# Pair 2's blocks fetched in step 4, queries and values loaded two steps later, batch 1's M a step later

## The chip, the cores and the metric

The kernel runs on one core of a Trainium2 chip. The metric is the device time of one execution in microseconds. Five engines work side by side, each through its own list of instructions in order: TensorE (PE, whose weight loads are shown apart as PEld), VectorE (DVE), ScalarE (ACT), GpSimd (POOL) and SyncE (SP). SP does no arithmetic here; it issues the DMAs.

## The reference

Two attentions follow each other: 32 packed rows for each head attend to the keys and values, and the queries attend to the packed result. Its output is the input of a two-layer block whose gate is `h * clip(h + 3, 0, 6) / 6`.

```python
def sm_attn(qq, kk, vv):
    s = scale * np.matmul(qq, kk.transpose(0, 1, 3, 2))
    s = s - np.max(s, axis=-1, keepdims=True)
    a = np.exp(s)
    a = a / (np.sum(a, axis=-1, keepdims=True) + 1e-09)
    return np.matmul(a, vv)
p_packed = sm_attn(p, k, v)
out = sm_attn(q, p_packed, p_packed)      # 8 batches, 8 heads, 576 rows, 64 wide
...
h = x @ w_in                              # x: 4608 x 512, w_in: 512 x 2048
relu6 = np.clip(h + 3.0, 0.0, 6.0)
g = h * relu6 / 6.0
return (g @ w_out).astype(np.float32)     # w_out: 2048 x 512
```

## The kernel before

**Tiling.** The eight batches are worked one after the other. The second attention's last product and the first layer are joined: with `A` the second attention's weights, `x @ w_in = A @ (p_packed @ w_in)`, and the product in brackets is called M. It is made in four quarters of 512 columns (`u_m`, tiles `m_hi` and `m_lo`: every number is kept as a rounded high part and a low rest). `first_product` (L930) multiplies M with `a_hi` and `a_lo` into `ps_hh`; ACT and DVE form the gate `t` or `tb` from it (`gate_into`, L946), ACT casts and DVE or POOL subtracts to get high and low parts (`parted`, L957), and PE multiplies them with the second layer's weights into `acc` (`product`, L975; its matmuls stand on L977).

**Steps.** From batch 1 on, a batch has two chunks (`c`) of 16 steps (`f`), one for each 128 hidden columns; `s = 16 * c + f` counts them through. Two neighbouring steps make a pair. For seven of the eight pairs (`PAIRS = 7`) the second product is done with seven half-width products in place of eight (`pair_product`, L1185), in the manner of Strassen, for which three combined weight blocks per pair, T1, T2 and T4, are kept ready in tiles `wt`. They are made once, during batch 1 and its turn to batch 2 (`combine`, L1068).

**Slots.** The `wt` tiles have room for the blocks of four pairs only. `PLACE` gives each pair its slot: pairs 2, 5 and 6 share slot 0, pairs 0 and 4 slot 1. Those five pairs' blocks are stored to `t_kept` in DRAM and fetched again, 768 KB each, by `fetch_t` (L1114, its DMA on L1115) in the steps that `FETCHES` names as (step, pair), one list for each chunk. In the first chunk the pairs come in the order 5, 4, 3, 2, 1, 0, 6. So pair 2's fetch waits until PE has done pair 5's product, and PE's product of pair 2 waits for the fetch. A pair's product is put behind the first products of the following pair (`pend`, `second`).

**The next batch's inputs.** While batch `b` is worked, `attention_inputs` (L566), one piece a step from step 0, loads the next batch's packed rows, keys, first two query blocks and values, and has DVE turn the keys (`turn`, L561). A block is four DMAs (`load_blocks`, L296, its DMA on L301). `nat`, the landing place of blocks, has two buffers, and `tr`, where the turned ones go, four. `attention` follows from step 6 (batch 1) or 10. `STAGES` sets these starts.

**M of the next batch.** The weights `w_in` are stored once to `w_kept`; `first_quarters` (L1418) fetches the quarters 2, 1 and 0 of them again into one single buffer (`w_again`, L1416) and makes M's quarters (`soon`, from step 21); the fourth is fetched at step 31 and used early in the next batch (`late`). The values `v_nat` use the same buffer.

**What sets the order.** The lists above only give the order in which the program is written and what a piece may not be put ahead of (`issue_after`, `behind_gates`). From batch 1 on a scheduler puts each engine's instructions in order by a time line of its own, SP's DMAs too. Once in order, an engine doesn't pass over an instruction that waits.

Of the kernel before, what the change touches and what calls it, by code (L numbers as in the profile page):

```python
# [34 lines left out]
TURN_LAST = (12, 12, 12, 13, 13, 14, 15)  # L35


FETCHES = (((5, 2), (7, 0), (11, 6)), ((5, 2), (7, 4), (11, 5)))
EDGES = (1, 2, 3)


# [43 lines left out]
def packed_attention_moe(  # L85
# [141 lines left out]
    def rest(*parts):  # L227
        for part in parts:
            for _ in part:
                pass  # L230

    def coarse(part):

        for stop in part:
            if stop is None:
                yield
# [59 lines left out]
    def load_blocks(src, b, a):  # L296
        t = ap.tile([P, T, 32], F32, name="nat", tag="nat", bufs=2)
        for h in range(2):
            for c in range(2):
                r = 64 * h + 32 * c  # L300
                nc.sync.dma_start(  # L301
                    out=t[r:r + 32],
                    in_=src[b, 2 * a + h, :, 32 * c:32 * c + 32].rearrange("(t i) j -> i t j", i=32),
                )
        return t
# [10 lines left out]
    def load_p(b):  # L316
        nat = ap.tile([P, NPAIR, NPK], F32, name="p_nat", tag="pn", bufs=1)
        for h in range(2):
            for c in range(2):
                r = 64 * h + 32 * c  # L320
                nc.sync.dma_start(
                    out=nat[r:r + 32],
                    in_=p[b, :, :, 32 * c:32 * c + 32].rearrange("(a h) i j -> h i a j", h=2)[h],
                )
        state["p", b] = nat

    def transpose_p(b):
        t = ap.tile([P, NPAIR, NPK], F32, name="p_tr", tag="pt", bufs=1)
        nc.vector.transpose(out=t, in_=state.pop(("p", b)))
        state["p", b] = t  # L330
# [90 lines left out]
    def load_v_low(b):  # L421

        home, tag = (wr, "w_in0") if steady else (wp, "v_nat")
        t = state["v", b] = home.tile([P, NPAIR, NST, D], F32, name="v_nat", tag=tag, bufs=1)
        for c in range(4):
            nc.sync.dma_start(out=t[:, :, c], in_=v[b].rearrange("(a x) r d -> x r a d", x=2)[0, c * P:(c + 1) * P])
        for x in range(2):
            load_v_rest(b, x)
# [107 lines left out]
    def u_m(b, *ns):  # L536
        def cols(n):
            return lambda a, half: w_in_sb[n][half, :, a]

        rounds = each_head(pps[b % 2], *(cols(n) for n in ns))  # L540
        yield
        for n, banks in reversed(list(zip(ns, rounds))):
            hi, lo = m_tiles(b, n)
            for x, ps in enumerate(banks):
                nc.scalar.copy(out=hi[:, x], in_=ps)
                yield 1
                nc.vector.tensor_sub(out=lo[:, x], in0=ps, in1=hi[:, x].bitcast(F32))
                yield

    def behind_gates():  # L550

        stack = ExitStack()
        for name in ("first", "relu", "gate"):
            if name in state:
                stack.enter_context(tc.issue_after(state[name].ins))
        return stack

    def load(which, b, a):
        state["nat", which, b, a] = load_blocks(k if which == "k" else q, b, a)

    def turn(which, b, a):  # L561
        t = ap.tile([P, T, 32], F32, name="tr", tag="tr", bufs=4)
        nc.vector.transpose(out=t, in_=state.pop(("nat", which, b, a)))  # L563
        state[which, b, a] = t

    def attention_inputs(b):  # L566

        load_p(b)
        load("k", b, 0)
        load("k", b, 1)  # L570
        yield
        transpose_p(b)
        turn("k", b, 0)
        load("k", b, 2)
        yield
        turn("k", b, 1)
        load("k", b, 3)
        yield
        turn("k", b, 2)
        load("q", b, 0)  # L580
        yield
        turn("k", b, 3)
        load("q", b, 1)
        load_v_low(b)
        yield
# [425 lines left out]
    def edge_product(acc, f, hi, lo, summed, first, last):  # L1011
# [11 lines left out]
        product(acc[:, H2:], lhs(2), block(i, "B22"))  # L1023

    def moe(b, chunks, fill):

        accs = {}
# [86 lines left out]
    def fetch_t(i):  # L1114
        nc.sync.dma_start(out=slots[PLACE[i]].rearrange("p a x m -> p (a x m)"), in_=t_kept[KEPT.index(i)])  # L1115
# [33 lines left out]
    def owed(count):  # L1149

        while ready and count:
            count -= 1
            ready.pop(0)()
            if edges:
                ready.append(edges.pop(0)())

    def moe_pairs(b, c, fill):

        last = PAIRS - 1
# [251 lines left out]
    def keep_w_in(n):  # L1411
        nc.sync.dma_start(out=w_kept[n], in_=w_in_sb[n].rearrange("p f a e -> p (f a e)"))

    def fetch_w_in(n):
        t = w_in_sb[n] = wr.tile([P, FPC, NPAIR, P], F32, name="w_again", tag="w_in0")
        nc.sync.dma_start(out=t.rearrange("p f a e -> p (f a e)"), in_=w_kept[n])  # L1416

    def first_quarters(b):  # L1418

        for n in range(NCH - 2, -1, -1):  # L1420
            fetch_w_in(n)
            yield
            yield
            yield from coarse(u_m(b, n))

    for b in range(1, B):
        more = b + 1 < B
        inputs, packed, ahead = (x(b + 1) if more else iter(()) for x in (attention_inputs, attention, u_s2))
        ahead = coarse(ahead)
        if b == 1:  # L1430
            late = coarse(part for n in range(1, NCH) for part in u_m(1, n))
            turned = [combine(i) for i in range(PAIRS)]
        else:
            late = coarse(u_m(b, NCH - 1))
        soon = first_quarters(b + 1) if more else iter(())

        def fill(c, f):
            s = c * NF + f
            with behind_gates():
                if b == 1:  # L1440
                    for _ in range(LATE[s] if s < len(LATE) else 0):
                        next(late, None)
                    if s == 0:
                        with tc.issue_after(state["stored"].ins):
                            for n in range(NCH):
                                keep_w_in(n)
                    for i in range(PAIRS - 1):
                        for _ in range(TURN[i].count(s)):
                            next(turned[i], None)
                else:  # L1450
                    if s > 0:
                        next(late, None)
                    for at, i in FETCHES[c]:
                        if f == at and (b, c, i) != (2, 0, PAIRS - 1):
                            fetch_t(i)
                    if b == 2:
                        for _ in range(TURN_LAST.count(s)):
                            next(turned[PAIRS - 1], None)
                if s >= 21:
                    next(soon, None)  # L1460
                if s == 31 and more:
                    rest(soon)
                    fetch_w_in(NCH - 1)
            with tc.issue_after(state["load"].ins), behind_gates():
                for chain, (start, count) in zip((inputs, packed, ahead), STAGES[b > 1]):
                    for _ in range(count if s >= start else 0):
                        next(chain, None)

        for c in range(2):
            if (b, c) == (1, 0):  # L1470
                moe(b, (c,), lambda f, c=c: fill(c, f))
                rest(*turned[:FIRST_PAIRS])
                roles.extend((3, 0, 1, 2))
            else:
                moe_pairs(b, c, lambda f, c=c: fill(c, f))
        if b == 1:
            rest(*turned[:PAIRS - 1])
# [31 lines left out]
```

## Time and profile before

| | |
|---|---|
| median of 3 runs | 720.52 us (720.29 to 721.84) |
| the profiled execution | 721.55 us |
| its span in the profile | 719.8 us |
| mean granted TensorE clock | 0.988 |
| DMA, 116.94 MB | mean 162 GB/s |

The span is what the profile shows of the profiled execution, from its first to its last instruction; the rest of the 721.55 us lies around it. In the prediction "us from the start" means from the start of the span. The batches from 2 on can be told apart in the time line by the two output DMAs (L1225) near their first steps, at 220.0, 300.2, 389.1, 468.7 and 558.8 us for batches 2 to 6.

### The profile page before, as it was taken

To read this page: it belongs to the slowest core of one execution; us is meant where nothing else is said; L and a number is where in the kernel's file an instruction comes from. 1 tells how busy PE (TensorE), PEld (TensorE's weight loads), DVE (VectorE), ACT (ScalarE), POOL (GpSimd) and SP (SyncE) were. 2 spreads that over 40 slices of the span, in tenths; PEclk is the share of its full clock that TensorE was granted. 3 is DMA by queue.
4 is the path that set the end of the run, shared out by engine and by line. 5 is a ranking of instruction groups with operands and counts; after the bars stand their busy time and mean duration, and the time that the engine had idled before them with its cause. 6 is when DMAs were issued, how large, how long until landed. Compare 5 with 4: busy or idle time off the path is not lost.

```text
span 719.8 us, 16493 instructions
## 1 busy us (share of the span) xinstructions
PE 691.9 (96%) x6014; PEld 599.8 (83%) x6014; DVE 552.8 (77%) x1227; ACT 436.8 (61%) x1042; POOL 364.5 (51%) x555
## 2 busy tenths in 40 slices
PE   7699999999999999999999999999999999999997
PEld 5487876788778888889898898889888898889996
DVE  4798688587999879876698778896688858986644
ACT  4798886555655656655466555566456655665543
POOL 1556642655444454574454444575634535467643
PEclk9699999999999999999999999999999999999999
DMA  9969953846247657564365756494544853532031
GB/s 277 321 167 274 208 131 145 241 106 179 76 160 166 158 169 253 135 189 88 115 249 144 191 112 223 153 208 114 130 162 162 180 146 138 201 132 89 30 109 68
DMA packets 200832, 116.94 MB, mean 162 GB/s; under 512 B 173616, under 2 KB 185392, under 8 KB 197168
## 3 DMA queue, kind: packets, MB, share of 16 engines
q1 hardware_dynamic: 200208, 115.70, 57.1%
q8 instruction: 47, 0.77, 0.4%
q14 instruction: 33, 0.27, 0.1%
q10 hardware_dynamic: 544, 0.20, 0.1%
HBM read 98.30 MB, written 17.56 MB: 161 GB/s over the span
## 4 chain that ended last, share of the span: by engine, by line
PE 72%; DVE 12%; DMA 8%; ACT 3%; issue 2%; SPq 2%; POOL 1%; DVEq 0%; ACTq 0%; POOLq 0%
PE acc L977 39%; PE ps_hh L937 19%; PE ps L357 4%; DMA wt<-t_kept 4%; PE ps_h L615 3%; DMA nat<-in_k_dram 2%; PE ps L977 2%; SPq L301 1%; PE ps L477 1%; DVE t L949 1%; DMA w_again<-w_kept 1%; DVE wt L1087 1%; DVE tr L563 1%; DMA raw_in<-in_moe_w_in_dram 1%; PE ps_t L686 1%
## 5 line engine op out<-in xcount | busy, mean ns | idle before, releaser
L955 POOL TENSOR_TENSOR gf<-tb,gf 128x256 fp32r<-128x256 f32 x87 | 74.2, 853 | 124.2 <-ACT gf L954 85.9
L937 PE MATMUL ps_hh<-a_hi,m_hi 128*128 128x320 f32 (+1 forms) x448 | 134.9, 301 | 1.6 <-PE acc L977 0.8
L937 PE MATMUL ps_hh<-a_lo,m_hi 128*128 128x320 f32 (+1 forms) x448 | 133.1, 297 | 0.0
L937 PE MATMUL ps_hh<-a_hi,m_lo 128*128 128x320 f32 (+1 forms) x448 | 132.9, 297 | 0.0
L949 DVE SCALAR_TENSOR_TENSOR t<-t,ps_hh 128x320 f32<-128x320 f32 (+1 forms) x137 | 60.8, 447 | 61.2 <-ACT t L948 60.3
L948 ACT ACTIVATE t<-ps_hh,three 128x320 f32<-128x320 f32 (+1 forms) x137 | 68.0, 500 | 46.8 <-PE ps_hh L937 42.9
L937 PEld LDWEIGHTS ps_hh<-a_hi,m_hi 128*128 128x128 f32 x448 | 84.9, 190 | 9.6 <-issue 2.0
L937 PEld LDWEIGHTS ps_hh<-a_lo,m_hi 128*128 128x128 f32 x448 | 85.0, 190 | 2.9 <-issue 0.9
L977 PE MATMUL acc<-wt,ga 128*128 128x256 f32 x522 | 87.2, 287 | 0.2 <-ACT ga L954 0.2
L937 PEld LDWEIGHTS ps_hh<-a_hi,m_lo 128*128 128x128 f32 x448 | 84.9, 190 | 1.3 <-issue 0.8
L977 PE MATMUL acc<-wo_hi,ge 128*128 128x256 f32 x348 | 82.6, 285 | 0.9 <-ACT ge L954 0.8
L977 PEld LDWEIGHTS acc<-wt,ga 128*128 128x128 f32 x522 | 72.7, 191 | 7.2 <-POOL bnd L973 2.5
L955 POOL TENSOR_TENSOR ga<-t,ga 128x256 fp32r<-128x256 f32 x87 | 69.6, 800 | 16.7 <-ACT ga L954 15.7
L977 PE MATMUL acc<-wo_hi,g 128*128 128x512 f32 x200 | 71.2, 398 | 0.0
L977 PEld LDWEIGHTS acc<-wo_hi,ge 128*128 128x128 f32 x348 | 61.0, 190 | 9.3 <-ACT gf L954 4.2
L977 PE MATMUL acc<-wt,gf 128*128 128x256 f32 x261 | 54.5, 286 | 6.7 <-DMA wt<-t_kept 6.7
L948 ACT ACTIVATE tb<-ps_hh,three 128x256 f32<-128x256 f32 (+1 forms) x87 | 43.4, 498 | 20.6 <-PE ps_hh L937 20.1
L973 POOL COPY bnd<-t 128x64 f32<-128x64 f32 x70 | 20.1, 286 | 64.0 <-DVE t L949 57.7
L563 DVE STREAM_TRANSPOSE tr<-nat 128x576 f32<-128x576 f32 x56 | 42.3, 764 | 11.4 <-DMA nat<-in_q_dram 5.0
L954 ACT CAST ge<-t 128x256 fp32r<-128x256 f32 x87 | 35.3, 405 | 25.0 <-DVE t L1239 23.4
L955 DVE TENSOR_TENSOR ge<-t,ge 128x256 fp32r<-128x256 f32 x87 | 42.3, 486 | 10.5 <-ACT ge L954 9.8
L954 ACT CAST gf<-tb 128x256 fp32r<-128x256 f32 x87 | 35.3, 405 | 24.0 <-DVE tb L949 22.4
(232 smaller groups left out, 1937.4 us busy)
## 6 DMA issues: line engine op xcount, KB each, us to landing
wt<-t_kept SPq DMA_DIRECT2D x35, 768.0 KB, 5.0
w_again<-w_kept SPq DMA_DIRECT2D x24, 1024.0 KB, 5.0
out_dram<-osb SPq DMA_DIRECT2D x33, 256.0 KB, 2.6
nat<-in_k_dram SPq DMA_DIRECT2D x112, 72.0 KB, 2.9
nat<-in_q_dram SPq DMA_DIRECT2D x112, 72.0 KB, 2.9
raw_in<-in_moe_w_in_dram SPq DMA_DIRECT2D x10, 512.0 KB, 5.9
raw_out<-in_moe_w_out_dram SPq DMA_DIRECT2D x10, 512.0 KB, 5.7
w_kept<-w_in_sb SPq DMA_DIRECT2D x4, 1024.0 KB, 9.2
```

Of the source, the lines that this page charges most:

```text
L301: nc.sync.dma_start(out=t[r:r + 32], in_=src[b, 2 * a + h, :, 32 * c:32 * c + 32].rearrange("(t i) j -> i t j", i=32),)
L357: nc.tensor.matmul(pair[x][NPK * a:NPK * a + NPK, :n], rows[half, a], c, start=True, stop=True)
L477: nc.tensor.matmul(pair[x][cols, :D], l, r, start=(c == 0), stop=(c == NST - 1))
L563: nc.vector.transpose(out=t, in_=state.pop(("nat", which, b, a)))
L615: nc.tensor.matmul(h[:, hf, :HS], mm[:, g, fs], aa[:, hf * HS:(hf + 1) * HS], start=(g == 0 and i == 0), stop=(g == NG - 1 and i == 2),)
L937: state["first"] = nc.tensor.matmul(h[:, :n], mm[:, g, fs], aa[:, t0:t0 + n], start=(g == 0 and i == 0), stop=(g == NG - 1 and i == 2),)
L948: state["relu"] = nc.scalar.activation(out=t[:, :n], in_=h, func=AF.Relu, bias=three)
L949: state["gate"] = nc.vector.scalar_tensor_tensor(out=t[:, :n], in0=t[:, :n], scalar=6.0, in1=h, op0=ALU.min, op1=ALU.mult)
L954: nc.scalar.copy(out=hi, in_=x)
L955: engine.tensor_sub(out=lo, in0=x, in1=hi.bitcast(F32))
L973: nc.gpsimd.tensor_copy(out=bnd[:, f, side * REM:side * REM + REM], in_=t[:, boff:boff + REM])
L977: nc.tensor.matmul(out, lhs[x], rhs[y], start=first and i == 0, stop=last and i == 2, skip_group_check=True)
```

## The change

Three lists of steps change:

- In the first chunk the blocks of pairs 2, 0 and 6 are asked for in steps 4, 6 and 10 in place of 5, 7 and 11; in the second chunk pair 2's in step 4 in place of 5.
- In `attention_inputs` the last key block is turned in the same step as before, but the first query block is loaded in step 5 in place of 3, the second and the values in step 6 in place of 4.
- In batch 1, the fetches of `w_in` and the making of batch 2's M start at step 22 in place of 21; from batch 2 on they stay at 21.

```diff
-FETCHES = (((5, 2), (7, 0), (11, 6)), ((5, 2), (7, 4), (11, 5)))
+FETCHES = (((4, 2), (6, 0), (10, 6)), ((4, 2), (7, 4), (11, 5)))
...
         load("k", b, 3)
         yield
         turn("k", b, 2)
+        yield
+        turn("k", b, 3)
+        yield
         load("q", b, 0)
         yield
-        turn("k", b, 3)
         load("q", b, 1)
         load_v_low(b)
         yield
...
-                if s >= 21:
+                if s >= (22 if b == 1 else 21):
                     next(soon, None)
```

**Where instructions move: SP in batch 4's first chunk.** Each row is the source line, the DMA with its tile and source, and how many follow each other. `nat` are the key and query blocks, `v_nat` the values, `wt` the fetched blocks of pairs 2, 0 and 6 in this order. Line numbers below 579 are the same in both kernels; later ones are two more in the changed one. Before:

```order
L301 DMA nat<-in_k_dram 32x18x32 x4
L301 DMA nat<-in_q_dram 32x18x32 x4
L426 DMA v_nat<-in_v_dram 128x4x64 x2
L301 DMA nat<-in_q_dram 32x18x32 x4
L416 DMA v_nat<-in_v_dram 64x4x64 x2
L1115 DMA wt_1788<-t_kept 128x1536
L1115 DMA wt_1789<-t_kept 128x1536
L1115 DMA wt_1788<-t_kept 128x1536
L301 DMA nat<-in_q_dram 32x18x32 x8
```

And in the changed kernel:

```order
L301 DMA nat<-in_k_dram 32x18x32 x4
L301 DMA nat<-in_q_dram 32x18x32
L1117 DMA wt_1771<-t_kept 128x1536
L301 DMA nat<-in_q_dram 32x18x32 x3
L426 DMA v_nat<-in_v_dram 128x4x64
L301 DMA nat<-in_q_dram 32x18x32 x2
L1117 DMA wt_1772<-t_kept 128x1536
L301 DMA nat<-in_q_dram 32x18x32 x2
L426 DMA v_nat<-in_v_dram 128x4x64
L416 DMA v_nat<-in_v_dram 64x4x64 x2
L1117 DMA wt_1771<-t_kept 128x1536
L301 DMA nat<-in_q_dram 32x18x32 x8
```

The three fetches stood together behind the queries and values. Now pair 2's stands behind one query DMA, and pair 0's and pair 6's are spread among the rest. Batches 3, 5 and 6 read alike; in batch 2 pair 2's fetch stands behind four query DMAs and ahead of all values.

**SP and DVE at the turn from batch 1 to batch 2.** `w_again` is the fourth quarter of `w_in`, for the last quarter of batch 2's M; `nat` are batch 3's keys. SP before, and then in the changed kernel:

```order
L1416 DMA w_again<-w_kept 128x2048 x2
L1111 DMA t_kept<-wt_1789 128x1536
L1416 DMA w_again<-w_kept 128x2048
L301 DMA nat<-in_k_dram 32x18x32 x4
L1225 DMA out_dram<-osb 128x512 x2
```

```order
L1418 DMA w_again<-w_kept 128x2048 x2
L1113 DMA t_kept<-wt_1772 128x1536
L301 DMA nat<-in_k_dram 32x18x32
L1418 DMA w_again<-w_kept 128x2048
L301 DMA nat<-in_k_dram 32x18x32 x3
```

The fetch moved behind the first of the four key DMAs. That key DMA waits until DVE has turned an earlier block out of its buffer (`tr<-nat`). DVE around that turning, before and then changed (`m_lo` is the subtraction of M's quarter, `t<-t,ps_hh` a gate, `wx` and `wo_lo` belong to `combine`):

```order
L547 TENSOR_TENSOR m_lo<-ps_2809,m_hi 128x512
L1087 TENSOR_TENSOR wt_1788<-wx,wt_1788 128x256
L949 SCALAR_TENSOR_TENSOR t<-t,ps_hh 128x256
L1105 TENSOR_TENSOR wx<-wo_hi,wx 128x256
L547 TENSOR_TENSOR m_lo<-ps_2809,m_hi 128x512
L1239 TENSOR_TENSOR t<-t 128x128
L329 STREAM_TRANSPOSE p_tr<-p_nat 128x128
L563 STREAM_TRANSPOSE tr<-nat 128x576
```

```order
L951 SCALAR_TENSOR_TENSOR t<-t,ps_hh 128x256
L1103 TENSOR_TENSOR wx<-wx,wo_lo 128x256
L1241 TENSOR_TENSOR t<-t 128x128
L329 STREAM_TRANSPOSE p_tr<-p_nat 128x128
L563 STREAM_TRANSPOSE tr<-nat 128x576
L1089 TENSOR_TENSOR wt_1771<-wx,wt_1771 128x256
L957 TENSOR_TENSOR ge<-t,ge 128x256
L1107 TENSOR_TENSOR wx<-wo_hi,wx 128x256
L547 TENSOR_TENSOR m_lo<-ps_2809,m_hi 128x512
```

Two subtractions of M and two steps of `combine` stood ahead of the turning and now stand behind it.

**PE at the same place.** The matmuls of M's last quarter (`ps<-w_again`, L357) followed four `ge` matmuls of pair 5's product before. In the changed kernel pair 5's product begins with six `ge` matmuls, and these rows follow them:

```order
L939 MATMUL ps_hh<-a_hi,m_hi 128x256
L939 MATMUL ps_hh<-a_lo,m_hi 128x256
L939 MATMUL ps_hh<-a_hi,m_lo 128x256
L939 MATMUL ps_hh<-a_hi,m_hi 128x256
L939 MATMUL ps_hh<-a_lo,m_hi 128x256
L939 MATMUL ps_hh<-a_hi,m_lo 128x256
L979 MATMUL acc<-wo_hi,gf 128x256
L979 MATMUL acc<-wo_lo,gf 128x256
L979 MATMUL acc<-wo_hi,gf 128x256
L979 MATMUL acc<-wt_1771,ga 128x256 x4
L979 MATMUL acc<-wt_1771,gf 128x256
L357 MATMUL ps_2883<-w_again,pps 32x512 x8
```

Between the start of the pair's product and M's last quarter stand 20 matmuls (6 and the 14 of these rows) where 4 stood. From batch 4 on PE's order is nearly that of before.

## The prediction

> **What bounds the kernel now.** I read the page's busy times first, then what TensorE (PE) waited for, then the time line around each of its waits on PE, SP, DVE, ACT and POOL, then the granted clock in half-microsecond stretches. The first fence has the page's row of busy times and one row of the view of waits (engine, line, what was waited for; us in total, times, longest).
>
> ```profile
> PE 691.9 (96%) x6014; PEld 599.8 (83%) x6014; DVE 552.8 (77%) x1227; ACT 436.8 (61%) x1042; POOL 364.5 (51%) x555
> ...
> PE acc L977 <- DMA wt<-t_kept: 6.7, 5, 1.9
> ```
>
> PE is busy for 691.9 of the 719.8 us of the span, so only about 28 us can be had without taking matmuls away, and this change takes none away. The largest single wait is that of the pair products (L977) for fetched blocks: 6.7 us in five places. The time line of PE shows the five (start, duration, what; in brackets the idle time ahead and what ended it):
>
> ```profile
> 238.14 0.62 PE L977 MATMUL acc<-wt,gf 128*128 128x256 f32 x3 [1.35 <-DMA wt<-t_kept]
> 317.03 0.62 PE L977 MATMUL acc<-wt,gf 128*128 128x256 f32 x3 [0.61 <-DMA wt<-t_kept]
> 406.33 0.62 PE L977 MATMUL acc<-wt,gf 128*128 128x256 f32 x3 [1.35 <-DMA wt<-t_kept]
> 486.38 0.62 PE L977 MATMUL acc<-wt,gf 128*128 128x256 f32 x3 [1.51 <-DMA wt<-t_kept]
> 576.51 0.62 PE L977 MATMUL acc<-wt,gf 128*128 128x256 f32 x3 [1.89 <-DMA wt<-t_kept]
> ```
>
> One wait stands in the first chunk of each of batches 2 to 6, the batches that also load the next batch's attention inputs; batch 7 loads none and has none. The first row of each wait is pair 2's T4, so it is pair 2's fetch into the shared slot that comes late. The five add up to 6.71 us.
>
> The last wait costs more than itself. These rows of the windows view give, for half a microsecond each, the busy time of PE, PEld, DVE, ACT and POOL, the granted TensorE clock, the DMA share and GB/s:
>
> ```profile
> 577.00:577.50 0.50, 0.50 (x5) 0.50 (x4) 0.15 (x1) 0.00 (x0) 0.00 (x0) 0.58 0.76 320
> 577.50:578.00 0.50, 0.50 (x4) 0.50 (x4) 0.00 (x0) 0.00 (x0) 0.00 (x0) 0.50 0.22 86
> ...
> 580.00:580.50 0.50, 0.50 (x5) 0.50 (x4) 0.27 (x1) 0.20 (x1) 0.00 (x0) 0.51 0.68 270
> 580.50:581.00 0.50, 0.50 (x6) 0.50 (x6) 0.47 (x2) 0.32 (x1) 0.00 (x0) 1.00 1.04 430
> ```
>
> The clock falls to half at about 577.1 and is whole again at about 580.5: 0.42 us of the first stretch, five stretches, 0.49 us of the last, 3.4 us in all, in which half the work is lost: 1.7 us. It begins 0.6 us after the 1.89 us wait ends; the four shorter waits are followed by none.
>
> **Why the fetch is late.** SP issues DMAs one after the other. Batch 4's piece of its time line, the last matmuls that read the slot for pair 5 (the fetch may not start before them), and the fetches' time from issue to landing:
>
> ```profile
> 391.24 2.32 SPq L301 DMA_DIRECT2D nat<-in_k_dram  x4
> 393.66 2.07 SPq L301 DMA_DIRECT2D nat<-in_q_dram  x4
> ...
> 397.67 2.06 SPq L301 DMA_DIRECT2D nat<-in_q_dram  x4
> ...
> 401.14 6.88 SPq L1115 DMA_DIRECT2D wt<-t_kept  x3
> ...
> 392.55 0.40 PE L977 MATMUL acc<-wt,ga 128*128 128x256 f32 x2
> ...
> DMA to landing us min/median/max: 4.2/5.0/8.3
> ```
>
> The slot is free at 392.95, but the fetch is issued at 401.14, behind two query blocks of four DMAs each and four value DMAs. It is the place in the queue that is late, not PE, and not the transfer.
>
> **The change, part by part.** *Pair 2's fetch.* No instruction is added or removed; the fetch now stands behind the last four key DMAs and one query DMA (batches 3 to 6) or four (batch 2). The key and query rows of the other batches:
>
> ```profile
> 223.47 3.02 SPq L301 DMA_DIRECT2D nat<-in_k_dram  x4
> 226.59 3.27 SPq L301 DMA_DIRECT2D nat<-in_q_dram  x4
> ...
> 232.37 0.55 SPq L1115 DMA_DIRECT2D wt<-t_kept  x1
> ...
> 302.40 2.33 SPq L301 DMA_DIRECT2D nat<-in_k_dram  x4
> ...
> 471.54 2.13 SPq L301 DMA_DIRECT2D nat<-in_k_dram  x4
> ...
> 560.89 2.35 SPq L301 DMA_DIRECT2D nat<-in_k_dram  x4
> ```
>
> One query DMA is a quarter of 2.07 us, 0.52 us. So the fetch is issued at 305.3, 394.1, 474.2 and 563.8 in batches 3 to 6 (start and duration of the key row, plus 0.52), and lands with the median 5.0 us at 310.3, 399.1, 479.2 and 568.8. PE asked (start of the waiting row less its wait) at 316.4, 405.0, 484.9 and 574.6: at least 5.7 us to spare, and still 2.4 us with the longest landing of 8.3. In batch 2 the fetch stands behind all four query DMAs, at 229.9 at the latest, lands at 234.9 and is wanted at 236.8; with 8.3 us it would be 1.4 us late. I take all five waits as gone: between 5.4 (batch 2's stays) and 6.7 us, and I take 6.7, because the median landing covers it.
>
> *Queries and values* move behind the fetch, in their own steps two later. What needs them first is the turning of the first query block on DVE, which stands behind the second half of the scores and not behind its own load:
>
> ```profile
> 410.60 1.44 DVE L563 STREAM_TRANSPOSE tr<-nat 128x576 f32<-128x576 f32 x2 [0.39 <-PE ps L357]
> ```
>
> In batch 4 the second query block's issue ended at 399.7 (397.67 and 2.06), 10.9 us ahead of that. Two fetches now stand ahead of parts of it, 0.55 us of issue for one in batch 2's row, and SP may be held for some microseconds by the second until pair 4's product is done. That stays inside the cover: I cost it at nothing; were the cover gone, DVE would wait first, not PE. The fetches of pair 0 and pair 6, asked for a step earlier, wanted PE's products of pairs 4 and 2 before and still do; no wait stood on them, nothing is gained.
>
> *What is late next in these chunks.* After the wait PE needs the gates of the next pair. Behind batch 4's wait, ACT and POOL stand idle until PE's next first product arrives:
>
> ```profile
> 408.48 0.48 ACT L948 ACTIVATE tb<-ps_hh,three 128x256 f32<-128x256 f32 x1 [1.46 <-PE ps_hh L937]
> ...
> 409.93 0.86 POOL L955 TENSOR_TENSOR gf<-tb,gf 128x256 fp32r<-128x256 f32 x1 [3.69 <-ACT gf L954]
> ```
>
> ACT's idle 1.46 us is as long as the 1.35 us that PE stood; without the stand both move forward together, and POOL has 3.69 us. So the gain is kept; the bounds are all of it and none of it.
>
> *Batch 1's M a step later.* This moves ACT and DVE work from one stage to the next at the change from batch 1 to 2, where the scheduler re-orders everything. The rows (windows as above; waits of PE; SP, DVE and the quarter's time to landing):
>
> ```profile
> 190.00:200.00 10.00, 9.00 (x68) 6.73 (x67) 10.00 (x19) 6.61 (x16) 4.79 (x7) 1.00 0.12 48
> ...
> 195.77 0.39 PE L977 MATMUL acc<-wo_hi,ga 128*128 128x256 f32 x1 [0.64 <-ACT ga L954]
> ...
> 217.61 0.38 PE L977 MATMUL acc<-wo_hi,ge 128*128 128x256 f32 x1 [0.59 <-ACT ge L954]
> ...
> 217.95 0.28 PE L977 MATMUL acc<-wo_hi,ge 128*128 128x256 f32 x1
> 218.07 0.28 PE L977 MATMUL acc<-wo_lo,ge 128*128 128x256 f32 x1
> ...
> 211.44 0.32 SPq L1416 DMA_DIRECT2D w_again<-w_kept  x1
> ...
> 216.24 0.68 DVE L547 TENSOR_TENSOR m_lo<-ps,m_hi 128x512 fp32r<-128x512 f32 x1
> ...
> 217.27 0.73 DVE L563 STREAM_TRANSPOSE tr<-nat 128x576 f32<-128x576 f32 x1
> ...
> DMA to landing us min/median/max: 4.7/5.0/8.8
> ```
>
> DVE is full there, and the two waits are for gates that stand behind other DVE work; in the new order DVE does two gates ahead of attention work and the M subtractions behind the first key block's turning. That can save the two waits, 1.2 us. Against it, the last quarter of the weights, issued at 211.44 before, now stands behind one key DMA that waits for that turning. If the turning ends at 218.0 as before, the quarter is issued at 218.5, a key DMA later, and lands at 223.5; PE, which is at pair 5's first product at 217.0 (217.61 less 0.59), comes to the quarter's matmuls 20 matmuls later, 0.12 us apart as in the two rows above, thus at 219.4. That is 4.1 us of new wait at most; with the M work taken out from ahead of the turning it ends earlier, by 0.68 us for each of two subtractions, and PE is held there by the gates anyway. Between a gain of 1.2 and a loss of 4.1, I take nothing: the gates, which pace this stage on both sides, are moved but not made fewer.
>
> **The sum.** The profiled execution took 721.55 us, 1.75 more than its span. Less 6.7 us of waits and 1.7 us of half clock: 713.1. The median of the three timed runs is 1.0 us below the profiled one, as a run without the clock's fall would be; less 6.7 alone it gives 713.8. I predict 713.4.
>
> [...]
>
> **The rivals.**
> - *The gain as summed*, 712.4 to 714.6: 57%. With the two waits at the change of batches gone as well, 712.2 or less: 5%.
> - *The last quarter of the weights is late*: a new wait of 1 to 4 us, 714.5 to 717.5: 14%. For it speaks the queue's order, against it that DVE is relieved ahead of the turning.
> - *The wait turns into one for gates*: PE, no longer standing, runs into ACT and POOL; half given back, 716.8: 9%. Against it stand the idle times above.
> - *The fall of the clock is not the wait's*: it stays, 721.55 - 6.7 = 714.9: 6%. Only its place right after the longest wait speaks against it.
> - *The change does not do what it says*: SP reaches the fetch early but is held, or the transfer is slowed by the loads beside it, and PE waits as long: 720.5: 5%. Against it the slot's freeing at 392.95.
> - *Slower*: the last quarter again, at its worst: key block turned at 218.0, landing with the longest time of its row, 8.8 us, at 227.3; PE stands 7.9 us and its clock falls twice, 3.4 us. That is 11.3 against 8.4 gained, 723.4. It decides from a landing later than about 226: 4%.
>
> 0.2% (1.4 us) is about what a measurement of this kernel can tell from no change. Faster by more: the first five cases less 1% each of the late quarter and of the gates, 89%; within: those and the unchanged wait, 7%; slower: 4%. The range from 711.6 (the 1.2 us saved and a little more) to 717.2 leaves out the late quarter's upper end and the last two cases.
>
> **What would show it.** Right: no row of PE waiting for wt, the fetch issued some 7 us earlier beside the same key rows, no half clock in batches 2 to 7, PE busy as before within 2 us. Wrong: PE waiting for w_again near 220, new waits for ACT's ga or ge in batches 2 to 6, or DVE idle ahead of the first query turning.

## The result and the profile after

The changed kernel takes 712.49 us (median of six executions, 709.84 to 714.10); the kernel before, run beside it, 720.69 us (718.43 to 724.79). The ratio is 0.9877, with a 95% interval from 0.9845 to 0.9909: 8.2 us faster. The profiled execution of the changed kernel took 714.10 us, with a span of 712.2 us.

The page's row of busy times, to lay beside the one of before:

```profile
PE 689.3 (97%) x6014; PEld 598.0 (84%) x6014; DVE 550.9 (77%) x1227; ACT 436.3 (61%) x1042; POOL 366.1 (51%) x555
```

PE does as many matmuls, in 2.6 us less. The view of PE's waits has no row for `wt` any more. After 122 us, outside the start-up, these are the largest that are left (engine, line, what was waited for; us in total, times, longest):

```profile
PE ps_hh L939 <- DVE tb L951: 1.3, 3, 0.6
...
PE ps L357 <- DMA w_again<-w_kept: 0.6, 1, 0.6
PE ps_hh L939 <- DVE t L951: 0.6, 1, 0.6
```

SP's time line in batch 4 (start, duration, line, DMA, count), which answers to the piece shown of before:

```profile
390.54 2.71 SPq L301 DMA_DIRECT2D nat<-in_k_dram  x4
393.35 0.49 SPq L301 DMA_DIRECT2D nat<-in_q_dram  x1
393.94 0.44 SPq L1117 DMA_DIRECT2D wt<-t_kept  x1
394.44 2.60 SPq L301 DMA_DIRECT2D nat<-in_q_dram  x3
...
409.26 4.29 SPq L301 DMA_DIRECT2D nat<-in_q_dram  x8
```

The fetch is issued at 393.94 where it was issued at 401.14. The view of the fetches' line has its time to landing, and the time line of PE the products that waited before in batches 2 and 4 (234.49 and 402.94), now with nothing in brackets behind them:

```profile
DMA to landing us min/median/max: 4.2/5.2/8.4
```

```profile
222.06 1.09 PE L357 MATMUL ps<-w_again,pps 64*32 64x512 f32 x16 [0.64 <-DMA w_again<-w_kept]
...
234.49 0.59 PE L979 MATMUL acc<-wt,gf 128*128 128x256 f32 x3
...
309.00 0.42 PE L939 MATMUL ps_hh<-a_hi,m_hi 128*128 128x320 f32 x1 [0.59 <-DVE tb L951]
...
402.94 0.52 PE L979 MATMUL acc<-wt,gf 128*128 128x256 f32 x3
```

The fetch of batch 4 by itself took 5.9 us to land, so the blocks were there at 399.8, 3.1 us ahead of the matmuls at 402.94. In batch 2 it was close: issued at 229.22 and landed 5.2 us later, at 234.4, the blocks came some 0.1 us ahead of the matmuls at 234.49. The other two rows are new waits that are worth a look: M's last quarter in batch 2, and a gate in batch 3.

The stretch of half clock behind batch 6's wait is gone. Two windows of batch 6 (busy times of PE, PEld, DVE, ACT and POOL, granted clock, DMA share, GB/s):

```profile
577.00:580.00 3.00, 3.00 (x28) 3.00 (x27) 1.49 (x6) 2.62 (x8) 0.00 (x0) 1.00 0.60 97
580.00:583.00 3.00, 2.77 (x24) 2.57 (x23) 2.63 (x8) 1.19 (x3) 1.03 (x2) 1.00 0.67 118
```

**Where the time went, stage by stage.** The output DMAs that mark the batches give the length of each stage; the second stage begins at a row of PE near 120 us that stands in all these profiles, a first product with 0.79 to 0.82 us of waiting for PE's own `acc`.

| from | before, us | after, us | gain, us | wait for `wt` and half clock there before, us |
|---|---|---|---|---|
| start to the row of PE | 120.07 | 121.37 | -1.30 | none |
| to batch 3 | 180.16 | 178.32 | 1.84 | 1.35 |
| batch 3 | 88.91 | 88.64 | 0.27 | 0.61 |
| batch 4 | 79.53 | 78.06 | 1.47 | 1.35 |
| batch 5 | 90.09 | 88.34 | 1.75 | 1.51 |
| batch 6 to the end | 161.04 | 157.47 | 3.57 | 1.89 + 1.7 |

Stage for stage the gain is what stood there as a wait, with 0.3 us given back in batch 3 (the gate above: 0.59 us new, 0.61 gone) and about 0.5 us more up to batch 3. The 1.3 us lost ahead of 120 us are scatter of the start-up, which the change doesn't touch: in the profiles of all the kernels below that row lies between 118.70 and 121.68, whatever was changed.

### The profile page after: what moved, and what is told of

It is laid out like the page before. It is cut to its first block, busy times and chain, and to the rows that moved or that the text cites. A ratio compares the mean times of both kernels' runs of the same rounds, so it can differ in the third digit from the quotient of the medians.

```text
span 712.2 us, 16486 instructions
## 1 busy us (share of the span) xinstructions
PE 689.3 (97%) x6014; PEld 598.0 (84%) x6014; DVE 550.9 (77%) x1227; ACT 436.3 (61%) x1042; POOL 366.1 (51%) x555
## 4 chain that ended last, share of the span: by engine, by line
PE 81%; DVE 7%; DMA 5%; ACT 3%; issue 2%; SPq 1%; POOL 0%; DVEq 0%; ACTq 0%; POOLq 0%
PE acc L979 44%; PE ps_hh L939 22%; PE ps L357 5%; PE ps_h L617 3%; DMA nat<-in_k_dram 2%; PE ps L979 2%; SPq L301 1%; PE ps L477 1%; DMA w_again<-w_kept 1%; PE ps L447 1%; DVE tr L563 1%; PE ps_t L688 1%; DMA raw_in<-in_moe_w_in_dram 1%; DMA raw_out<-in_moe_w_out_dram 1%; PE ps L280 1%
## 5 line engine op out<-in xcount | busy, mean ns | idle before, releaser
L957 POOL TENSOR_TENSOR g<-t,g 128x256 fp32r<-128x256 f32 x50 | 39.5, 793 | 20.4 <-ACT g L956 13.5
```

The source lines that it names most:

```text
L957: engine.tensor_sub(out=lo, in0=x, in1=hi.bitcast(F32))
```

## The experiments

Kernels before that ran beside the experiments had medians of 721.53 us (e1 to e4), 720.16 us (e5 to e8) and 723.04 us (e9 and e10); each ratio goes to its own.

### The fetch steps alone

```diff
-FETCHES = (((5, 2), (7, 0), (11, 6)), ((5, 2), (7, 4), (11, 5)))
+FETCHES = (((4, 2), (6, 0), (10, 6)), ((4, 2), (7, 4), (11, 5)))
```

> Only the three lists of FETCHES are changed; queries, values and batch 1's M stay as before. In the order pair 2's fetch then stands behind the four key DMAs and all four DMAs of the first query block, ahead of the values and the second query block: three query DMAs (3 x 0.52 = 1.6 us) later than in the changed kernel. Theory (the fetch's place in SP's queue is the whole gain, and 5 us of landing are covered): issued near 306.5, 395.5, 473.6 and 561.5 us in batches 3 to 6, none of the five waits for wt left, no half clock after one, time within 1.5 us of the changed kernel's 712.5. Rival (it is the later queries and values that free the fetch, and its own step does little): waits of about the old size remain in at least three batches, 717 us or more.

Measured: 714.24 us, ratio 0.9890 (0.9857 to 0.9923). SP's time line in batch 4, and the one row of PE in which a wait for `wt` is left, batch 2's:

```profile
392.12 2.62 SPq L301 DMA_DIRECT2D nat<-in_k_dram  x4
394.84 3.20 SPq L301 DMA_DIRECT2D nat<-in_q_dram  x4
398.14 0.44 SPq L1115 DMA_DIRECT2D wt<-t_kept  x1
```

```profile
237.38 0.62 PE L977 MATMUL acc<-wt,gf 128*128 128x256 f32 x3 [0.50 <-DMA wt<-t_kept]
```

The fetch passed the values and the second query block, not the first. That is enough for four batches; in batch 2 the fetch is issued as late as 232.31 and 0.50 us of the wait stays. So the expectation of no wait at all was missed there, and the time is 1.7 us above the changed kernel's where 1.5 was expected; the two ratios are not told apart.

### Queries and values alone

```diff
         turn("k", b, 2)
+        yield
+        turn("k", b, 3)
+        yield
         load("q", b, 0)
         yield
-        turn("k", b, 3)
         load("q", b, 1)
```

> Only the first two query blocks and the values are loaded two steps later; FETCHES and batch 1's M stay as before. In the order pair 2's fetch stands behind the four key DMAs and one query DMA in every batch, the same place as in the changed kernel from batch 3 on. Theory (place in SP's queue): the five waits are gone as with the whole change, 712.5 us within 1.5. Rival (the step in FETCHES is needed, SP being held behind something else): waits stay, 717 us or more.

Measured: 711.72 us, ratio 0.9865 (0.9829 to 0.9901), no wait for `wt`. SP in batch 4:

```profile
389.73 2.44 SPq L301 DMA_DIRECT2D nat<-in_k_dram  x4
392.27 0.44 SPq L301 DMA_DIRECT2D nat<-in_q_dram  x1
392.81 0.44 SPq L1117 DMA_DIRECT2D wt<-t_kept  x1
```

The fetch is asked for in the old step 5 and still stands where the whole change puts it, because what stood ahead of it has gone. So either edit alone brings nearly the whole gain, and the two do not add: both move the same fetch past the same DMAs.

### Batch 1's M alone, twice

```diff
-                if s >= 21:
+                if s >= (22 if b == 1 else 21):
```

> Only batch 1's fetches of w_in and its making of batch 2's M start a step later; FETCHES, queries and values stay as before. Theory (the M step nets nothing): five waits of PE for wt of 6 to 7 us in total as before, 720.7 us within 1.4; the two gate waits of 0.64 and 0.59 us at the change from batch 1 to 2 change places with a wait for w_again of about the same size. Rival (the M step gives a part of the measured 8.2 us of itself): 719 us or less with the five waits still there. Other rival (it costs, by the last quarter behind the key DMA): 722 us or more.

Measured: 719.37 us, ratio 0.9968 (0.9940 to 0.9996). The view of PE's waits:

```profile
PE acc L977 <- DMA wt<-t_kept: 5.4, 4, 1.6
...
PE ps L357 <- DMA w_again<-w_kept: 2.4, 2, 1.3
```

The waits for `wt` are there (batch 5 had none in this execution) and the weights' last quarter has become late, 1.03 us in batch 2; the other wait for weights, 1.3 us, stands at 282.56, at the making of batch 3's M. That the time fell by 0.3% none the less was not expected, so the kernel ran again:

> Batch 1's M alone a step later, once more, because the first time it was 0.3% faster (interval 0.04 to 0.60%) where no difference was expected. Theory (the M step nets nothing, the difference was the scatter of a kernel with waits of this length, in whose executions the half clock comes or not): within 0.2% of before, interval over 1. Rival (M later does gain by itself while the fetch is late): again 0.2 to 0.5% faster, with the interval below 1.

Measured: 719.70 us, ratio 0.9965 (0.9935 to 0.9995), in a profile with all five waits (6.7 us) and two stretches of half clock. My expectation failed: a small gain, by intervals that end just below 1, came twice. Neither profile shows where it comes from, and it isn't there once the fetch is early (next experiment). It stays open.

### The change without the M step

```diff
-                if s >= (22 if b == 1 else 21):
+                if s >= 21:
```

> The changed kernel with batch 1's M back at the old step. Theory (the M step nets nothing): 712.5 us within 1.4, no wait for wt, w_again's last quarter issued ahead of the key DMA again and no wait of PE for it, gate waits in its place. Rival (the M step gives part of the gain): 714.5 us or more. Other rival (it costs): 711 us or less.

Measured: 712.85 us, ratio 0.9884 (0.9854 to 0.9914). SP's time line at the turn from batch 1 to 2, and a row of PE in batch 2:

```profile
211.08 0.32 SPq L1418 DMA_DIRECT2D w_again<-w_kept  x1
217.66 1.96 SPq L301 DMA_DIRECT2D nat<-in_k_dram  x4
```

```profile
232.06 0.39 PE L939 MATMUL ps_hh<-a_hi,m_hi 128*128 128x256 f32 x1 [0.90 <-DVE t L951]
```

The last quarter is early again and PE doesn't wait for it; gates wait in its place, 0.65 and 0.59 us at the turn as before and 0.90 us here. With the early fetch the M step is worth nothing that can be measured.

### The change without the fetch steps

```diff
-FETCHES = (((4, 2), (6, 0), (10, 6)), ((4, 2), (7, 4), (11, 5)))
+FETCHES = (((5, 2), (7, 0), (11, 6)), ((5, 2), (7, 4), (11, 5)))
```

> The changed kernel with the old FETCHES: queries and values two steps later and batch 1's M a step later. In the order pair 2's fetch stands behind one query DMA from batch 3 on, as in the changed kernel. Theory (place in SP's queue): 712.5 us within 1.5, no wait for wt in batches 3 to 6, no half clock behind one. Rival (the three parts add up, each giving a share): 714.5 us or more.

Measured: 712.08 us, ratio 0.9847 (0.9821 to 0.9873), no wait for `wt`: the parts don't add up, they overlap. But the profile has a stretch of half clock at the turn to batch 2, where no wait is long. PE's rows with a wait, then two windows of 3.41 us, the length of the half clock in the first profile (577.07 to 580.48). Windows of this length, laid end to end from a change of the clock, are called pieces of a raster below:

```profile
218.99 0.39 PE L979 MATMUL acc<-wo_hi,gf 128*128 128x256 f32 x1 [0.22 <-POOL gf L957]
219.71 0.74 PE L979 MATMUL acc<-wt,ga 128*128 128x256 f32 x4 [0.33 <-ACT ga L956]
221.48 1.38 PE L357 MATMUL ps<-w_again,pps 64*32 64x512 f32 x16 [0.91 <-DMA w_again<-w_kept]
```

```profile
218.74:222.15 3.41, 1.95 (x23) 1.05 (x22) 3.41 (x8) 1.38 (x4) 1.66 (x3) 1.00 1.12 306
222.15:225.56 3.41, 3.41 (x21) 2.77 (x14) 2.42 (x6) 1.99 (x6) 1.88 (x3) 0.50 1.09 370
```

Three waits under a microsecond together leave PE busy for 1.95 of 3.41 us, and the next 3.41 us run at half clock. The changed kernel itself has the same three waits, 0.64 us in place of 0.91 for the weights, 2.22 us busy, and no half clock there.

### The kernel before, profiled again

> The kernel before, unchanged, for a second profile. Theory A (the clock is set on a raster of 3.41 us by what PE did in the raster's last stretch; in the first profile a stretch with PE busy for 1.52 us was followed by half clock, those with 1.95 us or more were not): the five waits stand again at 0.6 to 2 us; where they fall into the raster differs, so half clock follows each stretch after the start-up and ahead of PE's last work in which PE is busy for under about 1.5 us, and none in which it is busy for over 1.9; with waits this long that is none to two of them. Rival B (half clock has nothing to do with the waits): half clock in a place without a wait, or behind a stretch in which PE was busy for over 2 us.

> The kernel before, unchanged, for a third profile: as for the second. Theory A: none to two stretches of half clock, each behind a raster stretch with PE busy for under about 1.5 us. Rival B: half clock elsewhere.

Measured: spans of 720.4 and 717.1 us, five waits of 1.34, 1.03, 1.58, 1.59 and 1.57 us in the one, four of 0.54, 1.01, 1.84 and 0.94 us (none in batch 5) in the other. Each has one stretch of half clock, in batch 5 and in batch 4, where the first profile had it in batch 6. The windows on the raster in the first profile, the second and the third:

```profile
484.91:488.33 3.42, 1.95 (x15) 1.95 (x16) 1.53 (x4) 1.42 (x4) 2.40 (x4) 1.00 0.37 156
488.33:491.74 3.41, 3.41 (x38) 2.81 (x37) 2.23 (x6) 2.27 (x5) 1.27 (x3) 1.00 0.69 231
...
573.66:577.07 3.41, 1.52 (x13) 1.32 (x12) 2.41 (x7) 2.20 (x7) 1.96 (x3) 1.00 0.95 353
577.07:580.48 3.41, 3.41 (x18) 3.41 (x17) 0.33 (x2) 0.48 (x1) 0.00 (x0) 0.50 0.38 119
```

```profile
484.52:487.93 3.41, 1.82 (x25) 1.18 (x10) 2.46 (x6) 2.48 (x7) 2.44 (x6) 1.00 0.76 270
487.93:491.35 3.42, 3.42 (x16) 3.42 (x16) 0.00 (x0) 0.15 (x1) 0.34 (x1) 0.50 0.28 79
```

```profile
402.28:405.69 3.41, 1.57 (x13) 1.36 (x12) 2.41 (x7) 2.38 (x7) 2.07 (x4) 1.00 0.84 332
405.69:409.10 3.41, 3.41 (x18) 3.41 (x18) 0.43 (x1) 0.15 (x2) 0.00 (x0) 0.50 0.36 128
```

The falls of the second and the third profile came behind pieces with PE busy for 1.82 and 1.57 us. That fits theory A but for its bound of about 1.5 us, which was too low. M alone, run the second time, has two stretches in one execution, 92.16 us apart (485.92 and 578.08), which is 27 times 3.413 us:

```profile
482.50:485.92 3.42, 1.80 (x25) 1.16 (x10) 2.45 (x6) 2.49 (x7) 2.45 (x6) 1.00 0.69 262
485.92:489.33 3.41, 3.41 (x16) 3.41 (x16) 0.00 (x0) 0.10 (x1) 0.34 (x1) 0.50 0.27 76
574.66:578.08 3.42, 1.66 (x14) 1.46 (x14) 2.42 (x7) 2.29 (x7) 1.96 (x3) 1.00 0.93 363
578.08:581.49 3.41, 3.41 (x19) 3.41 (x18) 0.46 (x2) 0.47 (x1) 0.00 (x0) 0.50 0.29 86
```

### Longer waits: pair 2's fetch in pieces

The kernel before, with the first chunk's fetch for pair 2 in `n` DMAs, 4 in one kernel and 8 in the other.

```diff
-    def fetch_t(i):
-        nc.sync.dma_start(out=slots[PLACE[i]].rearrange("p a x m -> p (a x m)"), in_=t_kept[KEPT.index(i)])
+    def fetch_t(i, n=1):
+        for j in range(n):
+            to = slice(12 * P // n * j, 12 * P // n * (j + 1))
+            nc.sync.dma_start(out=slots[PLACE[i]].rearrange("p a x m -> p (a x m)")[:, to], in_=t_kept[KEPT.index(i)][:, to])
...
-                            fetch_t(i)
+                            fetch_t(i, 4 if (c, i) == (0, 2) else 1)
```

> The kernel before, with pair 2's fetch of the first chunk cut into four DMAs of 192 KB (same bytes, same place in the queue; in batch 2 four query DMAs come between the first piece and the rest). Three more issues of 0.33 us each make the last piece 1.0 us later, in batch 2 3.1 us. Theory (the wait is the fetch's place in the queue): waits of about 4.4, 1.6, 2.4, 2.5 and 2.9 us, 13.8 in place of 6.7. Theory A of the clock (a stretch of the 3.41 us raster with PE busy for under about 1.5 us is followed by half clock): two to four stretches of half clock, 1.7 us each, also behind waits under 3.4 us: together 720.7 + 7.1 + 1.7 to 5.1 = 729.5 to 733. [...] Rival C (the fall of before had another cause): none, 728 us or less.

Measured with four: 725.10 us, ratio 1.0059 (1.0026 to 1.0093). The waits for `wt` add up to 9.9 us in eight places; the largest rows, then two pieces of the raster with what follows them:

```profile
318.11 0.59 PE L977 MATMUL acc<-wt,gf 128*128 128x256 f32 x3 [1.95 <-DMA wt<-t_kept]
...
409.90 0.62 PE L977 MATMUL acc<-wt,gf 128*128 128x256 f32 x3 [1.78 <-DMA wt<-t_kept]
...
489.74 0.59 PE L977 MATMUL acc<-wt,gf 128*128 128x256 f32 x3 [1.75 <-DMA wt<-t_kept]
```

```profile
316.38:319.79 3.41, 1.68 (x13) 1.71 (x14) 1.32 (x4) 1.21 (x4) 2.19 (x4) 1.00 0.68 267
319.79:323.20 3.41, 3.41 (x38) 2.81 (x37) 2.23 (x6) 2.27 (x5) 1.27 (x3) 1.00 0.60 231
...
487.04:490.45 3.41, 1.66 (x19) 1.40 (x12) 2.45 (x6) 2.14 (x6) 2.43 (x5) 1.00 0.86 281
490.45:493.86 3.41, 3.41 (x17) 3.41 (x16) 0.00 (x0) 0.53 (x1) 0.00 (x0) 0.50 0.60 222
```

The waits grew, by 3.2 us and not by 7: PE now starts on a piece that has landed and waits again for the next. The time lies in the range of rival C alone (728 us or less), but that rival had no half clock, and one stretch came. The wait of 1.75 us is followed by half clock. The longer one of 1.95 us is not: it left 1.68 us busy in its piece of the raster where the other left 1.66.

> The same with eight DMAs of 96 KB: seven more issues, 2.3 us, in batch 2 4.4 us. Theory (place in the queue): waits of about 5.7, 2.9, 3.7, 3.8 and 4.2 us, 20 in all. Theory A of the clock: half clock behind four or five of them, 720.7 + 13.6 + 5.1 to 6.8 = 739 to 741. [...] Rival C: none, 735 us or less.

Measured with eight: 720.08 us, ratio 1.0003 (0.9982 to 1.0024): as before, where theory A had 739 to 741. The view of waits, and the view of the fetches' line:

```profile
PE acc L977 <- DMA wt<-t_kept: 2.9, 4, 1.4
```

```profile
DMA to landing us min/median/max: 1.9/2.4/8.2
```

The median landing of the fetches, most of them now pieces of 96 KB, falls from 5.0 to 2.4 us, so PE starts earlier. PE is busy for 692.8 us without any half clock, against 691.9 before with one stretch of it; that it stops for short times between the pieces, hidden in the durations of its rows, is my reading and isn't shown. Cutting the fetch also changed PE's order around it: 98 of its 6014 matmuls stand in other places than before with four pieces, 174 with eight. Rival C's forecast (no half clock, 735 us or less) came out, but all the forecasts rested on longer waits. The experiment doesn't lengthen the waits as meant and says nothing on the clock.

## Why the prediction was right, point by point

**The five waits (right, 6.7 us).** All five are gone. The fetches were issued at 229.22, 304.99, 393.94, 472.07 and 559.93, in batches that began up to 4.0 us earlier than before. Measured from each batch's output DMAs that is 0.2 to 0.7 us later than predicted (10.23 against 9.9, 5.30 against 5.1, 5.61 against 5.0, 5.68 against 5.5, 5.20 against 5.0): the key DMAs ahead took 2.71 us in batch 4 in place of 2.32. The five landed after 5.2, 5.6, 5.9, 5.5 and 6.9 us, all later than the median of 5.0 that the prediction took. In batches 3 to 6 the cover held all the same. In batch 2 the 1.9 us of cover (234.9 to 236.8) shrank to about 0.1, since PE came to the product at 234.49: that this wait went too is in part luck. That the place in SP's queue is the cause is shown by the two single edits, which have nothing in common but that place. Over the profiles, with the fetch late (before three times, M alone twice) 23 of 25 places have the wait; with it early (the change, each of the two edits alone, the change without M's step and without the fetch steps) 1 of 25 has.

**The half clock (right, 1.7 us).** The prediction tied it to the longest wait because it stood right behind it. In the profiles it goes with the waits, not with the longest one of a run alone: of the seven stretches after the start-up six came behind a wait for `wt` (1.59, 1.62, 1.75, 1.76, 1.84 and 1.89 us) and the seventh behind three short waits (0.22, 0.33 and 0.91 us). The profiled execution of the changed kernel has none after the start-up; the others were not profiled, and the kernel without the fetch steps had one behind other waits.

**The sum, closed on all profiles.** Take each profile's time from the row of PE near 120 us to the end of the span, less the waits for `wt`, less 1.7 us for each stretch of half clock:

| profile | from the row to the end, us | waits for `wt`, us | half clock, us | rest, us |
|---|---|---|---|---|
| before | 599.7 | 6.7 | 1.7 | 591.3 |
| before, second | 600.9 | 7.1 | 1.7 | 592.1 |
| before, third | 598.2 | 4.3 | 1.7 | 592.2 |
| M alone | 597.2 | 5.4 | 0 | 591.8 |
| M alone, again | 600.8 | 6.7 | 3.4 | 590.7 |
| changed | 590.8 | 0 | 0 | 590.8 |
| fetch steps alone | 592.9 | 0.5 | 0 | 592.4 |
| queries and values alone | 591.6 | 0 | 0 | 591.6 |
| changed, M as before | 592.5 | 0 | 0 | 592.5 |
| changed, fetches as before | 591.5 | 0 | 1.7 | 589.8 |

The first column spreads over 10 us, the last over less than 3: these two terms are what tells the kernels apart. With the fetch in four or eight pieces the rest is 593.5 and 595.5 us, where PE's order differs and part of the waiting between pieces may lie inside rows that count as busy.

**The number (0.9 us too high: 713.4 against 712.49).** The 0.9 us lie inside the interval of the ratio, which is 709.5 to 714.1 us, so the number alone doesn't decide between the two sums of the prediction. The profiles speak against the second one. I read the median's lying 1.0 us below the profiled execution as runs without the half clock, took only the 6.7 us from it, and so got 713.8. All three profiles of before have one stretch of half clock, also the third, whose 718.86 us lie below that median. Less both terms the median gives 720.52 - 8.4 = 712.1, an estimate, since the terms differ from one execution to the next (4.3 us of waits in the third profile).

**Queries and values later (right).** Alone they cost nothing: 711.72 us. In the changed kernel DVE does stand longer for query blocks, 7.3 us in seven places where it was 5.0 in six, and no row of PE waits for it:

```profile
DVE tr L563 <- DMA nat<-in_q_dram: 7.3, 7, 1.8
```

None of the seven stands ahead of a batch's first query turning, the sign of being wrong that the prediction named: they stand ahead of the third or fourth query block, whose loads' steps the change left alone.

**Gates next (right, with a small return).** In batch 3 a wait of 0.61 us went and a gate's wait of 0.59 us came; the stage kept 0.27 us. Elsewhere the gain was kept.

**Batch 1's M (right as a sum, in the changed kernel).** The last quarter is issued at 216.58, 1.9 us ahead of the worst case of 218.5, because the turning came earlier once M's subtractions stood behind it; PE waits 0.64 us for it in place of 4.1 at most. So a sign of being wrong, PE waiting for `w_again` near 220, did come, in a size that cost nothing in sum. No run has a wait of 7.9 us there, so the two falls of the clock that the slower rival adds for it are not shown by any run; behind the 0.64 us the clock stayed whole. With and without the step: 712.49 and 712.85. That the step gives some 2 us alone, with the fetch late, was not predicted, and its cause isn't known.

**One sign of being right missed.** PE's busy time was to stay within 2 us and fell by 2.6. The half clock that went, 1.7 us, counts in it; the prediction had not taken it off there, and the rest was not traced.

**A better version** did not come out: queries and values alone (711.72), the change without the fetch steps (712.08) and the change itself (712.49) are not told apart.

## What to carry to other kernels

When a transfer is late, look first at what its queue issues ahead of it: here, in batch 4, the slot was free 8 us earlier, and moving either the fetch forward or its neighbours back brought nearly the whole gain, so that a second edit for the same wait brings nothing. Price a wait of PE with the half clock that can come behind it (here 1.7 us behind six of the nine waits of 1.59 us or more), and add up neighbouring short waits before calling them harmless: here three of 0.22, 0.33 and 0.91 us within 3.41 us had half clock behind them. Judge such a gain by closing the account on several profiles (time, less waits, less half clock), because the executions scatter (718.43 to 724.79 us before, 709.84 to 714.10 changed).

## What the runs showed of the hardware

In the first profile the granted clock rises at 37.77, falls at 577.07 and rises at 580.48; 577.07 - 37.77 is 158 times 3.413. The two falls in the second profile of M alone, 92.16 us apart, are 27 times 3.413 apart. After the start-up and ahead of the last matmuls, all seven stretches of half clock followed a piece of the raster with PE busy for 1.52 to 1.95 us (1.52, 1.57, 1.66, 1.66, 1.80, 1.82, 1.95). Between 1.68 and 1.95 us both came: pieces with 1.68 (fetch in four pieces), 1.84 (before's second profile) and 1.95 us (its first) had full clock behind them.

So these profiles draw no sharp bound by PE's modelled busy time, and the length of the longest wait is not far behind as a sign: of the nine waits for `wt` of 1.59 us or more, six were followed by half clock, and one of 1.59 and those of 1.78 and 1.95 were not. What speaks for the busy time in a piece is the fall behind the three short waits, and that two of the waits without a fall lie across a border of the raster: the 1.59 us (M alone, again) from 403.09 to 404.68 across 404.00, with 2.50 and 2.73 us busy in the two pieces, and the 1.78 us (fetch in four pieces) from 408.12 to 409.90 across 408.54 (487.04 less 23 times 3.413).

Among the ten pieces under 2 us named here the weight loads (PEld) tell the two kinds apart: at most 1.46 us busy ahead of half clock, 1.63 or more where the clock stayed. This was seen afterwards and is not tested; in the first profile a piece with PE busy for 3.00 us kept its clock with weight loads of 1.23 us (116.27 to 119.68).

In the start-up half clock also followed a piece with PE busy for 2.4 us (the change without the fetch steps, 17.36 to 20.77), and in the first profile two pieces with 2.32 and 3.41 us that ran at half clock themselves (from 24.11 and from 30.94), so nothing of this is shown for other mixes of work.

The three profiles of before have their half clock in batches 6, 5 and 4, behind waits of 1.89, 1.59 and 1.84 us; that it depends on how a wait falls on the borders is my reading of the rows above and isn't shown by itself. Each of the seven stretches lasted one piece, 3.41 us, at half the clock, thus 1.7 us.

With pair 2's fetches of the first chunk cut into eight pieces of 96 KB the median landing of all fetches was 2.4 us, against 5.0 us where all were whole blocks of 768 KB; PE waited 2.9 us for them in place of 6.7, but the kernel took 720.08 us, a ratio of 1.0003.
